# Seven output products with four sums, in tiles 1 to 8: another form of the fast output product in a sparse-attention and bilinear-FFN kernel

## The chip, the cores and the metric

The kernel runs on one core of a Trainium2 chip. The metric is the device time of one execution in microseconds (us); the median of the runs is compared. PE is the matrix engine, PEld its weight load, DVE the vector engine, ACT the scalar engine, POOL the GpSimd engine and SP the engine that issues DMAs.

## The reference

The inputs are q, k, v of shape (8, 8, 576, 64) and the weights w_a, w_b (512 x 1536) and w_out (1536 x 512), all in float32.

```python
scores = scale * np.matmul(q, k.transpose(0, 1, 3, 2))
mask_local = (rel >= 0) & (rel < 32)
mask_strided = (rel >= 0) & (pos[None, :] % 32 == pos[:, None] % 32)
scores = np.where(masks, scores, -1e9)      # first 4 heads local, last 4 strided
attn = softmax(scores); attn_out = attn @ v
x = attn_out.transpose(0, 2, 1, 3).reshape(4608, 512)
out = ((x @ w_a) * (x @ w_b)) @ w_out       # 4608 x 512, float32
```

## The kernel before

The 4608 tokens are cut into nine tiles (t = 0 to 8) of 512 tokens, and a tile into 16 slots, numbered 16t to 16t+15. In slots 0 to 11 (`ffn_ab`, f = 0 to 11) PE makes 128 columns of d_ff of `x @ w_a` and `x @ w_b` in two PSUM banks a and b, four matmuls of 512 columns each (L581). ACT copies a to SBUF (L598), and DVE multiplies it with b into `pf[:, f]` (L601 where the tile uses the fast output product, with the tokens sorted into two halves; L603 elsewhere). Slots 12 to 15 make the output, `pf` times `w_out`.

The plain output product (`ffn_y`, tiles 0 and 1) makes 4 x 12 matmuls of 512 columns (L768). Each of the four results is copied by ACT (L777) and stored. The fast one (`ffn_ys`, tiles 2 to 8, named by `FAST_Y`) sees the output as two by two blocks: two halves of the tokens (i), two halves of the 512 output columns (j), and the two halves (e) of each pair of d_ff chunks. Seven products of 128 x 256 blocks replace eight. Each has 2 x 6 matmuls of 256 columns (q = two interleaved sets of tokens, g = six chunk pairs; L686), 84 a tile. Some operands are sums: `wf` holds sums of weight blocks, made once by `fast_w` (L175), and `pss` holds sums of `pf` blocks, made in each tile by `fast_s` (L614 to L618) on DVE. `y_plan` runs this for tiles 2 to 7 and `y_tail` for tile 8. `post` moves the products out of four banks a, b, c, d in the order 3, 4, 1, 7, 5, 2, 6: three ACT copies (L658, L669, L671), four DVE additions (L662, L665, L667, L675), and two POOL subtractions that are put into slots 16t+15 and 16t+17 (L881 is where `do` queues them).

The banks of `mm_bank` go round: three buffers of the pool "mm" and one of "tp", so every fourth request gets the same bank. A request waits until all readers of the bank's last contents are done.

The attention of the later batches is mixed in between the matmuls. A table (`STEPS` for batches 1 and 2, `LATER` for 3 to 7) gives the slot of each step, relative to 16(b-1). A step S makes scores on PE (L385), Exp on ACT (L393) and a mask on DVE (L403). A step V makes `o` on PE (L486), Ln and Exp of the sums on ACT (L495, L496), and two multiplications into `xT` on DVE (L500 or L502). Both have one PSUM tile for all steps. `step_D` transposes q and k of a coming batch on DVE (L327, L332). Steps with a .5 position run in the middle of a slot. In the output phase each of the four slots takes 21 matmuls from the generator, with the step of a .5 position after 11 of them; slot 15 takes the rest. For tiles 2 to 6 the steps around the output phase are V4 after slot 9, S6 after 10, V5 after 11, S7 after 12, V6 within 13, V7 after 14, and S0 of the next batch after 15. In tile 1, V4, V5, V6, V7 lie within slots 28, 29, 30, 31, and S6, S7 after 28 and 29.

The order on every engine is that of the program (`manual_schedule`). The main loop runs a slot, then what `soon` holds for it, then the table's steps (`take(i)`), then what `at` holds for it, in the order in which it was put in:

```python
            done = fn(t, j, mid) if fn is not ffn_ab else fn(t, j, mid, first.get(j) if t == 0 else None)
            if i > 13 and i in at and done is not None:
                nc.gpsimd.tensor_copy(pace, done)
            for f in soon.get(i, ()):
                f()
            take(i)
            for f in at.get(i, ()):
                f()
```

The copy into `pace` (L936) holds POOL, and with it the loads that POOL issues, until the slot's result is there.

Of the kernel before, what the change touches and what calls it, by code (L numbers as in the profile page):

```python
# [7 lines left out]
F32 = mybir.dt.float32  # L8
# [18 lines left out]
FAST_Y = (2, 3, 4, 5, 6, 7, 8)  # L27
# [3 lines left out]
def kernel(  # L31
# [136 lines left out]
    wf = wp.tile([128, 5, FG, HN], BF16, name="wf")  # L168
    wov = wo_sb.rearrange("p (g e) (j n) -> p e j g n", e=2, j=2)

    def fast_w(n, gs):
        a, b, op = ((wov[:, 0, 1], wov[:, 1, 1], ALU.subtract), (wov[:, 1, 0], wov[:, 0, 0], ALU.subtract),
                    (wov[:, 0, 0], wov[:, 1, 1], ALU.add), (wov[:, 0, 0], wov[:, 0, 1], ALU.add),
                    (wov[:, 1, 0], wov[:, 1, 1], ALU.add))[n]
        nc.vector.tensor_tensor(wf[:, n, gs], a[:, gs], b[:, gs], op=op)  # L175
# [349 lines left out]
    def step_X(b, c):  # L525
# [17 lines left out]
                 12.6: "S1", 12.75: "L0 X2", 13: "s2 X3 V0 m2 L1 W3", 13.5: "V1 S3 W4", 14: "V2 X0", 14.5: "V3 D1", 15: "X1"},  # L543
# [64 lines left out]
    def fast_s(t, n, gs):  # L608
        if t not in pss:
            pss[t] = nat.tile([128, FG * 5 * SW], BF16, tag="shared", name="ps").rearrange("p (n g m) -> p n g m", g=FG, n=5)  # L610
        s = pss[t][:, :, gs, :HT]
        x = pfs[t].rearrange("p (g e) (i m) -> p e i g m", e=2, i=2)[:, :, :, gs]
        if n == 0:
            nc.vector.tensor_tensor(s[:, 0], x[:, 0, 0], x[:, 1, 1], op=ALU.add)  # L614
        elif n == 1:
            nc.vector.tensor_tensor(s[:, 1:3], x[:, 0], x[:, 1], op=ALU.add)
        else:
            nc.vector.tensor_tensor(s[:, 3:], x[:, :, 1], x[:, :, 0], op=ALU.subtract)  # L618
# [4 lines left out]
    def products(t):  # L623
        pf, s = pfs[t], pss[t]
        full = lambda e, i: (lambda g, q: pf[:, 2 * g + e, HT * i + q:HT * (i + 1):2])
        summed = lambda n: (lambda g, q: s[:, n, g, q:HT:2])
        wsum = lambda n: (lambda g: wf[:, n, g])
        wfull = lambda e, j: (lambda g: wov[:, e, j, g])
        return {"3": ("a", full(0, 0), wsum(0)), "4": ("b", full(1, 1), wsum(1)), "1": ("c", summed(0), wsum(2)),
                "2": ("b", summed(2), wfull(0, 0)), "5": ("a", summed(1), wfull(1, 1)), "6": ("c", summed(3), wsum(3)),  # L630
                "7": ("d", summed(4), wsum(4))}

    def f32t(nm):
        return fsb.tile([128, 2, HN], F32, tag=nm, name=nm, bufs=1)
# [10 lines left out]

    def y_plan(t):

        plan, bank, v = products(t), {}, {}
        y = []

# [4 lines left out]
        def post(k):  # L655
            if k == "3":
                v["a"] = v["w"] = f32t("ya")
                nc.scalar.copy(v["a"], bank["a"])  # L658
                y.extend(y_bufs())
                v["y"] = y  # L660
            elif k == "4":
                nc.vector.tensor_tensor(v["w"], bank["b"], v["a"], op=ALU.add)  # L662
            elif k == "1":
                v["e"] = f32t("ye")
                nc.vector.tensor_tensor(v["e"], bank["c"], v["w"], op=ALU.add)  # L665
            elif k == "7":
                nc.vector.tensor_tensor(v["e"], v["e"], bank["d"], op=ALU.subtract)  # L667
            elif k == "2":
                nc.scalar.copy(y[1][:, :, col(0)], bank["b"])  # L669
            elif k == "5":  # L670
                nc.scalar.copy(y[0][:, :, col(1)], bank["a"])  # L671
                do(16 * t + 15, nc.gpsimd.tensor_tensor, y[0][:, :, col(0)], v["e"], y[0][:, :, col(1)], ALU.subtract)
                do(16 * t + 18, store_half, 0)
            else:
                nc.vector.tensor_tensor(v["w"], bank["c"], v["w"], op=ALU.add)  # L675
                do(16 * t + 17, nc.gpsimd.tensor_tensor, y[1][:, :, col(1)], v["w"], y[1][:, :, col(0)], ALU.subtract)
                do(16 * t + 19, store_half, 1)

        for k in "3417526":
            b, lhs, rhs = plan[k]  # L680
            new = b not in bank
            if new:
                bank[b] = mm_bank([128, 2, HN])
            for q in range(2):
                for g in range(FG):
                    nc.tensor.matmul(bank[b][:, q], lhsT=lhs(g, q), rhs=rhs(g), start=new and q == 0 and g == 0,  # L686
                                     stop=g == FG - 1, skip_group_check=True)
                    if g == FG - 1 and q == 1:
                        post(k)
                    yield v  # L690

    def y_tail(t):

        plan, y = products(t), y_bufs()
        w, e = f32t("ya"), f32t("ye")
        v = {"a": w, "y": y}
        for q in range(2):
            if q == 0:
                bank = {x: mm_bank([128, HN]) for x in "abcd"}
            else:  # L700
                bank = {"a": psum4["o"].tile([128, 2, 512], F32, tag="o", name="end")[:, 0, :HN],
                        "b": pst.tile([128, 2, 512], F32, tag="st", name="end")[:, 0, :HN],
                        "c": mm_bank([128, HN]), "d": mm_bank([128, HN])}
            c21, c12, c22 = y[1][:, q, col(0)], y[0][:, q, col(1)], y[1][:, q, col(1)]
            wq, eq = w[:, q], e[:, q]
            seen = set()
            for k in ("3415267", "3412567")[q]:
                b, lhs, rhs = plan[k]
                cuts = [(slice(0, HN), bank[b])]
                if (k, q) == ("7", 1):  # L710
                    cuts = [(slice(0, 128), bank[b][:, :128]), (slice(128, HN), mm_bank([128, 128]))]
                for n, dst in cuts:
                    for g in range(FG):
                        nc.tensor.matmul(dst, lhsT=lhs(g, q), rhs=rhs(g)[:, n], start=g == 0 and b not in seen,  # L714
                                         stop=g == FG - 1, skip_group_check=True)
                        if g < FG - 1:
                            yield v
                    if k == "3":
                        nc.scalar.copy(wq, bank["a"])
                    elif k == "4":  # L720
                        nc.vector.tensor_tensor(wq, bank["b"], wq, op=ALU.add)
                        if q == 0:
                            fast_s(t, 1, slice(FG - 1, FG))
                    elif k == "1":
                        nc.vector.tensor_tensor(eq, bank["c"], wq, op=ALU.add)
                        if q == 0:
                            fast_s(t, 2, slice(FG - 1, FG))
                    elif k == "2":
                        nc.scalar.copy(c21, bank["b"])
                        nc.gpsimd.tensor_tensor(wq, wq, c21, op=ALU.subtract)  # L730
                        if q == 1:
                            y_store(nc.sync, t, y, 1, q, col(0))
                    elif k == "5":
                        nc.scalar.copy(c12, bank["a"])
                        nc.gpsimd.tensor_tensor(eq, eq, c12, op=ALU.subtract)
                        if q == 1:
                            y_store(nc.scalar, t, y, 0, q, col(1))
                    elif k == "6":
                        nc.vector.tensor_tensor(c22, bank["c"], wq, op=ALU.add)
                        y_store(nc.sync, t, y, 1, q, col(q) if q else slice(0, d_model))  # L740
                    else:
                        nc.vector.tensor_tensor(y[0][:, q, n], eq[:, n], dst, op=ALU.subtract)
                        if q == 0:
                            y_store(nc.sync, t, y, 0, q)
                        else:
                            y_store(nc.scalar if n.start == 0 else nc.sync, t, y, 0, q, n)
                    yield v
                seen.add(b)

    def ffn_ys(t, j, mid):  # L750
        if j == 0:
            yst[t] = (y_tail if t == NT - 1 else y_plan)(t)
        for i in range(21):
            v = next(yst[t])
# [5 lines left out]
        return (v["a"][:1, 0, :1], None, v["y"][0][:1, 0, HN:HN + 1], v["y"][1][:1, 0, :1])[j]  # L760
# [36 lines left out]
    with tc.manual_schedule(engines={ENG.PE, ENG.SP, ENG.Pool, ENG.DVE, ENG.Activation}):  # L797
# [85 lines left out]
        soon = {16 * t + 11: [lambda t=t: fast_s(t, 0, slice(2, 6))] for t in FAST_Y[:-1]}  # L883
# [34 lines left out]
        for n, slot in enumerate((16, 16, 19, 20, 22)):  # L918
            do(slot, fast_w, n, slice(3, 6))
        for g in range(FG):  # L920
            for n in range(3 if g < FG - 1 else 1):
                do(16 * (NT - 1) + 2 * g + 1, fast_s, NT - 1, n, slice(g, g + 1))
        for t in FAST_Y[:-1]:
            for slot, n, z0, z1 in ((4, 0, 0, 2), (6, 2, 0, 2), (8, 1, 0, 2), (10, 2, 2, 4), (11, 2, 4, 6),
                                    (12, 1, 2, 6)):
# [44 lines left out]
```

## Time and profile before

| | |
|---|---|
| median of 3 runs | 328.86 us (328.71 to 328.89) |
| span of the profiled execution, first to last instruction | 326.3 us; its own device time is not given apart from the runs |
| mean granted PE clock | 0.999 |
| PE busy | 320.6 us (98%) |
| DVE busy | 265.7 us (81%) |
| ACT busy | 202.7 us (62%) |
| POOL busy | 177.2 us (54%) |
| output phases: tile 1 / tile 3 / tile 7 | 80.17 to 92.11 / 150.19 to 160.16 / 283.19 to 292.36 us |

The profile is of one execution. Each row of a timeline gives the start in us from the span's start, the duration, the engine, the line, the operation and its tiles; what stands in square brackets is idle time ahead of it and what ended it. Rows of one engine overlap a little, so the step from one start to the next is the cost in a full queue. PE matmuls are pipelined: a row of 0.27 us for 256 columns follows its predecessor by 0.11 us.

### The profile page before, as it was taken

To read this page: it belongs to the slowest core of one execution; us is meant where nothing else is said; L and a number is where in the kernel's file an instruction comes from. 1 tells how busy PE (TensorE), PEld (TensorE's weight loads), DVE (VectorE), ACT (ScalarE), POOL (GpSimd) and SP (SyncE) were. 2 spreads that over 40 slices of the span, in tenths; PEclk is the share of its full clock that TensorE was granted. 3 is DMA by queue.
4 is the path that set the end of the run, shared out by engine and by line. 5 is a ranking of instruction groups with operands and counts; after the bars stand their busy time and mean duration, and the time that the engine had idled before them with its cause. 6 is when DMAs were issued, how large, how long until landed. Compare 5 with 4: busy or idle time off the path is not lost.

```text
span 326.3 us, 7676 instructions
## 1 busy us (share of the span) xinstructions
PE 320.6 (98%) x2820; PEld 205.5 (63%) x2820; DVE 265.7 (81%) x509; ACT 202.7 (62%) x329; POOL 177.2 (54%) x295
## 2 busy tenths in 40 slices
PE   8999999999999999999999999999999999999995
PEld 6754655455555587557999985569555954584474
DVE  6766888889778999999999999999877845647562
ACT  6764775478778765777677757875677643313321
POOL 8935839599966655875577557853312031232021
PEclk9999999999999999999999999999999999999999
DMA  9999999999999798799979999898033022004004
GB/s 151 154 204 201 204 184 182 173 171 136 132 213 116 95 97 79 77 217 125 83 72 199 138 86 77 160 180 84 20 77 115 2 67 64 0 2 129 1 2 129
DMA packets 98869, 37.50 MB, mean 115 GB/s; under 512 B 76688, under 2 KB 96016, under 8 KB 98832
## 3 DMA queue, kind: packets, MB, share of 16 engines
q0 software_dynamic: 85968, 19.48, 64.5%
q1 hardware_dynamic: 12576, 17.34, 18.4%
q8 instruction: 22, 0.36, 0.4%
q10 hardware_dynamic: 288, 0.20, 0.2%
q14 instruction: 15, 0.12, 0.1%
HBM read 39.51 MB, written 9.44 MB: 150 GB/s over the span
## 4 chain that ended last, share of the span: by engine, by line
PE 96%; DMA 2%; POOL 0%; DVE 0%; issue 0%; POOLq 0%; ACT 0%; DVEq 0%
PE mm L581 56%; PE mm L686 17%; PE mm L768 6%; PE st L385 5%; PE o L486 4%; DMA shared<-in_q_dram 2%; PE mm L714 2%; PE o L442 1%; PE ab L581 1%; PE misc L154 1%; PE tp L511 1%; PE tp L296 1%; PE end L714 1%; PE tp L287 0%; POOL shared L197 0%
## 5 line engine op out<-in xcount | busy, mean ns | idle before, releaser
L581 PE MATMUL mm<-xT,wa_sb 128*128 128x512 bf16 (+1 forms) x472 | 110.3, 357 | 0.0
L581 PE MATMUL mm<-xT,wb_sb 128*128 128x512 bf16 (+1 forms) x472 | 110.3, 357 | 0.0
L598 ACT COPY a_sb<-mm 128x512 f32<-128x512 f32 x106 | 62.1, 586 | 48.3 <-PE mm L581 47.6
L936 POOL CAST pace<-pf 1x1 f32<-1x1 bf16 x84 | 31.4, 374 | 84.0 <-DVE pf L601 80.7
L581 PEld LDWEIGHTS <-wb_sb 128*128 128x128 bf16 x480 | 46.3, 98 | 44.0 <-issue 0.2
L601 DVE TENSOR_TENSOR pf<-a_sb,mm 128x512 bf16<-128x512 f32 x84 | 56.4, 672 | 17.0 <-PE mm L581 13.8
L581 PEld LDWEIGHTS <-wa_sb 128*128 128x128 bf16 x480 | 42.7, 98 | 31.3
L393 ACT ACTIVATE p<-st 128x576 bf16<-128x576 f32 (+1 forms) x64 | 41.6, 650 | 11.7 <-PE st L385 11.1
L495 ACT ACTIVATE xr<-o 64x576 f32<-64x576 f32 x48 | 31.1, 649 | 25.0 <-PE o L486 24.2
L686 PEld LDWEIGHTS <-ps 128*128 128x128 bf16 x360 | 34.6, 98 | 3.9
L496 ACT ACTIVATE xr<-xr 64x576 f32<-64x576 f32 x48 | 32.9, 685 | 1.5
L500 DVE TENSOR_TENSOR xT<-o,xr 64x288 bf16<-64x288 f32 x48 | 21.5, 447 | 7.2 <-ACT xr L496 6.7
L502 DVE TENSOR_TENSOR xT<-o,xr 64x288 bf16<-64x288 f32 x48 | 21.5, 448 | 6.2 <-ACT xr L496 5.1
L686 PE MATMUL mm<-wf,ps 128*128 128x256 bf16 x216 | 26.4, 273 | 0.0
L768 PE MATMUL mm<-wo_sb,pf 128*128 128x512 bf16 x96 | 23.4, 379 | 0.0
L403 DVE TENSOR_TENSOR p<-p,mask_l 128x576 int16<-128x576 int16 x32 | 22.2, 694 | 1.2 <-ACT p L393 1.1
L243 POOL DMA_DIRECT2D vs<-in_v_dram x24 | 19.7, 821 | 3.0 <-PE st L385 2.2
L212 POOL DMA_DIRECT2D kl<-in_k_dram x24 | 16.1, 671 | 5.5 <-issue 3.6
L212 POOL DMA_DIRECT2D ql<-in_q_dram x24 | 16.0, 666 | 5.2 <-DMA wo_sb<-in_moe_w_out_dram 3.8
L603 DVE TENSOR_TENSOR pf<-a_sb,mm 128x512 bf16<-128x512 f32 x22 | 14.9, 676 | 4.3 <-ACT a_sb L598 2.8
L936 POOL COPY pace<-y_sb 1x1 f32<-1x1 f32 x16 | 2.8, 177 | 27.8 <-ACT y_sb L669 15.1
L686 PE MATMUL mm<-wf,pf 128*128 128x256 bf16 x144 | 17.6, 273 | 0.0
(162 smaller groups left out, 502.1 us busy)
## 6 DMA issues: line engine op xcount, KB each, us to landing
out_dram<-y_sb SPq DMA_DIRECT2D x12, 512.0 KB, 4.6
out_dram<-y_sb SPq DMA_DIRECT2D x10, 256.0 KB, 3.3
vl<-in_v_dram POOLq DMA_DIRECT2D x6, 384.0 KB, 6.8
kl<-in_k_dram POOLq DMA_DIRECT2D x24, 72.0 KB, 3.0
ql<-in_q_dram POOLq DMA_DIRECT2D x24, 72.0 KB, 3.0
vs<-in_v_dram POOLq DMA_DIRECT2D x24, 72.0 KB, 3.7
wo_sb<-in_moe_w_out_dram POOLq DMA_DIRECT2D x4, 384.0 KB, 9.2
natk<-in_k_dram POOLq DMA_DIRECT2D x20, 72.0 KB, 3.3
```

Of the source, the lines that this page charges most:

```text
L212: nc.gpsimd.dma_start(out=t[32 * h:32 * h + 32], in_=src[b, h].rearrange("(i y) d -> y i d", y=32))
L393: nc.scalar.activation(p[:M, :, :W], st[:M, :, :W], ACT.Exp, scale=scale)
L403: nc.vector.tensor_tensor(pi, pi, mk, op=ALU.bitwise_and)
L495: nc.scalar.activation(r, sums, ACT.Ln)
L496: nc.scalar.activation(r, r, ACT.Exp, scale=-1.0)
L500: nc.vector.tensor_mul(dst[:, W * half:W * (half + 1)], o[:64, j, :W], r[:, j])
L581: nc.tensor.matmul(ps_[:, c0:c0 + n], lhsT=w[:, kk, 128 * f:128 * (f + 1)], rhs=xT[:, kk, x0:x0 + n], start=(kk == first and c0 == 0), sto ...
L598: nc.scalar.copy(a_sb, ab[0])
L601: nc.vector.tensor_mul(pf[:, f, :].rearrange("p (i a s) -> p a i s", i=2, s=16), halves(a_sb), halves(ab[1]))
L686: nc.tensor.matmul(bank[b][:, q], lhsT=lhs(g, q), rhs=rhs(g), start=new and q == 0 and g == 0, stop=g == FG - 1, skip_group_check=True)
L768: nc.tensor.matmul(ybank[j], lhsT=pf[:, f, 128 * j:128 * (j + 1)], rhs=wo_sb[:, f], start=(f == 0), stop=(f == FD - 1))
L936: nc.gpsimd.tensor_copy(pace, done)
```

## The change

The fast output product is used in tile 1 too. Its form is another. Instead of five sums of `pf` blocks and five of weight blocks there are four of each, some made from an earlier sum, and all are subtractions or additions of two blocks. Three PSUM banks X, Y, Z take the seven products in the order 1, 7, 6, 4, 5, 2, 3, where X holds 1, then 1+6, then 1+6+5, then 1+6+5+3, and is copied by ACT at each of these points; Z holds 7, copied, and then 7+4; Y holds 2. A tile's output phase thus has five ACT copies and three DVE additions, one of them (after 5) from SBUF alone, and no POOL subtraction. The places of the sums in the slots change: s0, s2, s1 of the first four chunk pairs are made after slots 8, 9, 10, the last two pairs of s2, s0, s1 directly after slot 11's `pf`, and s3 after slots 11 and 12. The tail tile mixes the products of q = 0 and q = 1.

```diff
-FAST_Y = (2, 3, 4, 5, 6, 7, 8)
+FAST_Y = (1, 2, 3, 4, 5, 6, 7, 8)
...
-    wf = wp.tile([128, 5, FG, HN], BF16, name="wf")
+    wf = wp.tile([128, 4, FG, HN], BF16, name="wf")
...
+        a, b = ((wov[:, 0, 1], wov[:, 0, 0]), (wov[:, 1, 1], wf[:, 0]), (wov[:, 1, 1], wov[:, 0, 1]),
+                (wov[:, 1, 0], wf[:, 1]))[n]
+        nc.vector.tensor_tensor(wf[:, n, gs], a[:, gs], b[:, gs], op=ALU.subtract)
...
-        if n == 0:
-            nc.vector.tensor_tensor(s[:, 0], x[:, 0, 0], x[:, 1, 1], op=ALU.add)
-        elif n == 1:
-            nc.vector.tensor_tensor(s[:, 1:3], x[:, 0], x[:, 1], op=ALU.add)
-        else:
-            nc.vector.tensor_tensor(s[:, 3:], x[:, :, 1], x[:, :, 0], op=ALU.subtract)
+        a, b, op = ((x[:, 0, 1], x[:, 1, 1], ALU.add), (s[:, 0], x[:, 0, 0], ALU.subtract),
+                    (x[:, 0, 0], x[:, 0, 1], ALU.subtract), (x[:, 1, 0], s[:, 1], ALU.subtract))[n]
+        nc.vector.tensor_tensor(s[:, n], a, b, op=op)
...
+        return {"1": ("X", full(0, 0), wfull(0, 0)), "2": ("Y", full(1, 0), wfull(1, 0)), "3": ("X", summed(3), wfull(1, 1)),
+                "4": ("Z", full(1, 1), wsum(3)), "5": ("X", summed(0), wsum(0)), "6": ("X", summed(1), wsum(1)),
+                "7": ("Z", summed(2), wsum(2))}
...
+    def y_post(k, y, q, bank, n=slice(0, HN)):
+        part = lambda i, j: y[i][:, q, HN * j:HN * (j + 1)]
+        if k in "1765":
+            nc.scalar.copy({"1": part(0, 0), "7": part(0, 1), "6": part(1, 0), "5": part(1, 1)}[k], bank)
+        if k == "4":
+            nc.vector.tensor_tensor(part(1, 0), bank, part(1, 0), op=ALU.add)
+        elif k == "5":
+            nc.vector.tensor_tensor(part(1, 1), part(1, 1), part(0, 1), op=ALU.add)
+        elif k == "2":
+            nc.vector.tensor_tensor(y[0][:, q, n], bank, y[0][:, q, n], op=ALU.add)
+        elif k == "3":
+            nc.scalar.copy(part(0, 1), bank)
...
+        bank = {x: mm_bank([128, 2, HN]) for x in "YXZ"}
...
-        for k in "3417526":
+        for k in "1764523":
             b, lhs, rhs = plan[k]
             for q in range(2):
                 for g in range(FG):
+                    nc.tensor.matmul(bank[b][:, q], lhsT=lhs(g, q), rhs=rhs(g), start=k in "172" and q == 0 and g == 0,
                                      stop=g == FG - 1, skip_group_check=True)
                     if g == FG - 1 and q == 1:
+                        y_post(k, y, slice(0, 2), bank[b])
+                    yield y
+        do(16 * t + 18, store_half, 0)
+        do(16 * t + 19, store_half, 1)
...
+        for q, k in ((0, "1"), (0, "7"), (0, "6"), (0, "4"), (0, "5"), (1, "1"), (0, "3"), (1, "7"), (1, "6"), (0, "2"),
+                     (1, "5"), (1, "4"), (1, "3"), (1, "2")):
...
-        return (v["a"][:1, 0, :1], None, v["y"][0][:1, 0, HN:HN + 1], v["y"][1][:1, 0, :1])[j]
+        return (y[0][:1, 0, :1], None, y[1][:1, 0, HN:HN + 1], y[1][:1, 0, :1])[j]
...
-        soon = {16 * t + 11: [lambda t=t: fast_s(t, 0, slice(2, 6))] for t in FAST_Y[:-1]}
+        soon = {16 * t + 11: [lambda t=t, n=n: fast_s(t, n, slice(4, 6)) for n in (2, 0, 1)] for t in FAST_Y[:-1]}
...
-            for slot, n, z0, z1 in ((4, 0, 0, 2), (6, 2, 0, 2), (8, 1, 0, 2), (10, 2, 2, 4), (11, 2, 4, 6),
-                                    (12, 1, 2, 6)):
+            for slot, n, z0, z1 in ((8, 0, 0, 4), (9, 2, 0, 4), (10, 1, 0, 4), (11, 3, 0, 4), (12, 3, 4, 6)):
                 do(16 * t + slot, fast_s, t, n, slice(z0, z1))
```

In the table of steps for batch 1 the fifth weight sum's step (W4) goes, and so does its second half in slot 22.

## The prediction

> **What bounds the kernel now.** I read the page first: the busy shares, and the chain that ended last.
>
> ```profile
> PE 320.6 (98%) x2820; PEld 205.5 (63%) x2820; DVE 265.7 (81%) x509; ACT 202.7 (62%) x329; POOL 177.2 (54%) x295
> ...
> PE 96%; DMA 2%; POOL 0%; DVE 0%; issue 0%; POOLq 0%; ACT 0%; DVEq 0%
> ```
>
> PE is the path for 96% of the span. The waits view shows under 2 us of PE waiting in all, and the PE timeline has no hole inside a tile. So less PE work is gained one for one, and every new PE wait is lost one for one. Next I took the windows of three output phases (columns: window and its length, then busy time and count of PE, PEld, DVE, ACT, POOL, clock, DMA share, GB/s): tile 1 with the plain product, tile 5 and tile 7 with seven products.
>
> ```profile
> 80.20:92.10 11.90, 11.90 (x97) 6.16 (x96) 8.65 (x17) 8.60 (x15) 10.00 (x15) 1.00 1.34 140
> ...
> 218.65:228.60 9.95, 9.95 (x112) 8.99 (x111) 9.71 (x18) 6.42 (x10) 4.94 (x9) 1.00 0.70 77
> ...
> 283.40:292.50 9.10, 9.10 (x85) 8.12 (x84) 5.19 (x7) 1.76 (x3) 2.35 (x4) 1.00 0.01 2
> ```
>
> Where attention steps are mixed in (tile 5) DVE is full; in tile 7, where they have ended, it is half empty. What decides is thus whether DVE and ACT meet the deadlines that the new form sets in tiles 1 to 6.
>
> **The gain.** In the PE timeline six plain 512-column matmuls of L768 take 80.17 to 81.46 us, 0.216 each, 48 of them 10.38 us. Twelve 256-column ones (L686, 291.05 to 292.36) take 1.31, so one takes 0.109 and a product of twelve 1.31; 84 take 9.17. Tile 1 gains 1.21 us. Tiles 2 to 8 keep 84: no PE gain.
>
> **Three new deadlines.** (a) Before, four banks served seven products, and a bank came back after three others; now X is used by products 1, 6, 5, 3, with only one product (1.31 us) between 1 and 6, between 6 and 5, and between 5 and 3, and PE must wait until ACT has copied X. (b) The banks go round in a ring of four, so Y, X, Z are the banks of f=10's a, f=10's b, f=11's a. The first product needs X: DVE must have done pf of f=10 when the phase begins; before, that bank was the second product's. The second product now needs sum s2, whose last two groups come after pf of f=11. (c) Y is read last by a DVE addition, and the next tile's first b product takes that bank.
>
> **Tile 5 as the pattern of 2 to 5.** From the DVE timeline (start, duration):
>
> ```profile
> 216.11 0.91 DVE L502 TENSOR_TENSOR xT<-o,xr 64x288 bf16<-64x288 f32 x2
> 217.05 0.78 DVE L327 STREAM_TRANSPOSE tq<-ql 128x576 bf16<-128x576 bf16 x1
> 217.75 0.65 DVE L601 TENSOR_TENSOR pf<-a_sb,mm 128x512 bf16<-128x512 f32 x1
> 218.33 0.44 DVE L403 TENSOR_TENSOR p<-p,mask_s 72x576 int16<-72x576 int16 x1
> 218.69 0.68 DVE L618 TENSOR_TENSOR ps<-pf 128x1024 bf16<-128x1024 bf16 x1
> 219.29 0.68 DVE L601 TENSOR_TENSOR pf<-a_sb,mm 128x512 bf16<-128x512 f32 x1
> 220.00 0.69 DVE L614 TENSOR_TENSOR ps<-pf 128x1024 bf16<-128x1024 bf16 x1
> ```
>
> PE begins the phase at 218.48. The multiplications of step V4 start when ACT's Exp is done, in all these tiles 2.37 to 2.41 us before the phase. DVE is in order, so work saved ahead of them doesn't help what follows. Slot 9 now adds s2 of four groups ahead of pf of f=10. A sum of 128x1024 takes 0.61 from start to start (218.69 to the next row), so pf starts at 217.75+0.61=218.36 and ends at 219.01. No row shows what PE needs after that; the bounds are 0 and 0.15 (ACT starts 0.02 after its own last row, and 0.2 after PE), and I take 0.05. Product 1 starts at 219.06: **0.58 lost**. Mask 218.94, s1 of four groups for L618's place 219.30, pf of f=11 219.90, s2's last 512 columns 0.71 later (219.29 to 220.00) and 0.41 long (L614's 128x512 form): 221.02, with 0.05 221.07. PE wants it 16 matmuls after its start, at 219.06+1.75=220.81: **0.26**.
>
> ACT in the same tile, and the end of the phase on DVE:
>
> ```profile
> 222.70 0.65 ACT L495 ACTIVATE xr<-o 64x576 f32<-64x576 f32 x1 [0.81 <-PE o L486]
> 223.38 0.69 ACT L496 ACTIVATE xr<-xr 64x576 f32<-64x576 f32 x1
> ...
> 226.37 0.65 ACT L495 ACTIVATE xr<-o 64x576 f32<-64x576 f32 x1
> ```
>
> ```profile
> 228.72 0.71 DVE L332 STREAM_TRANSPOSE tk<-natk 128x512 bf16<-128x512 bf16 x1
> 229.35 0.65 DVE L675 TENSOR_TENSOR ya<-mm,ya 128x512 f32<-128x512 f32 x1
> ```
>
> Step V6 lies four matmuls before product 6 ends; PE goes on from it at 222.50. Its Ln and Exp stand ahead of the copy of 6 on ACT: Exp ends at 224.07, the copy (0.59) at 224.68, PE may go on at 224.73. Product 5 would start 4+12 matmuls after 222.50, at 224.25: **0.48**. (The copy of 7 has Exp of S7 ahead of it and is done 0.4 early; the copy of 5 is ahead of V7's Ln, early too.) PE goes on from V7 at 226.15. The addition of 2 takes the place of L675, behind V7's multiplications and L332, at 229.35, done 230.00, with 0.05 230.05. The next tile's b product begins at 229.35: **0.70**. Sum 2.02 a tile, 8.1 for four, since each wait comes after the one before and nothing on PE takes it back.
>
> **Tile 6** has no transposes. V4 starts at 250.13, 0.94 later s2, then pf of f=10 ends at 252.33, before the phase at 252.51: nothing. s2's end, by the same rows 254.41, against 254.26: 0.15. The copy of 6: 0.48. The addition of 2 straight behind V7's multiplications, 3.25 after V7 against 2.94 (21 matmuls' 2.29 and 0.65): 0.31. Sum 0.94.
>
> **Tile 7** has only copies on ACT: the copy of 6 is done 0.5 early; s2 at 1.45 against 1.75. Nothing.
>
> **Tile 1** is new to the sums, and DVE there is late already. pf of f=10 and f=11 now start at 79.42 and 81.97; s0 and s2 come ahead of the first, s1 too ahead of the second. First: 79.42+1.22=80.64, done 81.29, product 1 at 81.34 against 80.17: 1.17. Second: 81.97+1.83=83.80, s2 from 84.51 to 84.92, against 81.34+2.00 (16 matmuls and V4's 0.26): 84.97, 1.63. V4's multiplications stand behind s2, s0, s1 (0.33 each), a transpose (0.76) and s3 (0.61): 86.87 to 87.80. Step V5 needs its PSUM tile at 86.97: 0.86. Copies behind Ln and Exp: 0.22 and 0.16, V7's tile 0.1. Waits 4.14, less the gain 1.21: +2.93.
>
> **Tail (tile 8).** The same 84 matmuls; 0.13 for s2's last group (DVE 314.36 against 314.28), the copies of 128x256 take 0.37 and end some 0.02 to 0.3 before their bank is wanted. The last addition and two 64 KB stores stay. I take 0.1, with bounds -0.2 (the addition of L742 no longer stands behind L739) and +0.5 (a 128 KB store's issue of 0.61 ahead of the last on ACT's queue).
>
> **What costs nothing.** Five copies for three on ACT (+1.17 a tile; ACT 62%), one addition from SBUF alone (no row; 0.35 to 0.69 by half and whole of L662; DVE waits for Exp behind it), a fifth weight sum less (2x0.55), pace copies of slots 14 and 30 behind that addition: loads that land in 3 us and are used slots later. Two POOL subtractions a tile go (1.27 each). Beside one of them the mask L403 took 1.97 us in place of 0.44, so 1.5 of DVE come back at a tile's start; V4's wait for Exp swallows it.
>
> [...]
>
> **Sum:** 8.1+0.94+2.93+0.1=12.1. The span of 326.3 is 2.6 under the median of the runs, 328.86, taken as fixed: 328.86+12.1=341.0.
>
> **Rivals.** *Only ACT's waits are real* (0.14): the DVE relief reaches the deadlines after all. Then 5x0.48=2.4 in tiles 2 to 6 and 0.54+0.22+0.16=0.9 for the copies of 1, 6 and 5 in tile 1, less 1.21: 331.0. For it: a tile's sums fall from 5.0 us of DVE (L614's 0.42 and 0.69, three of L618 and one of L616 at 0.68, L616's 1.19) to 4x0.69+4x0.42=4.4, its additions by 0.7, and the 1.5. Against it: V4 starts on Exp in each tile. *Faster* (0.09): X's copies come in time, because ACT reaches the copy of 6 before V6's Ln, and DVE is ahead: 328.86-1.21=327.65. The place is product 5 in tiles 2 to 6; it decides where that wait is under 0.2 a tile and DVE's under 0.05. The code order speaks against it. *The waits do more* (0.12): PE is slow to restart, 0.15 rather than 0.05 at some 24 waits (+2.4), and late steps push the next tile's: 345 to 348. The clock is 1.00 in every window of the trace.
>
> [...]
>
> *No change* (0.03): waits just eat the 1.21.
>
> **Numbers.** The forecast holds 0.62. Its own range: without (c) and the 0.05s about 337, with 0.15 each 343.5. For eight in ten I reach to the ACT rival and a part of the worse one: 331 to 345. 0.2% (0.66 us) is about what a measurement tells from none; faster 0.09, within 0.03, slower 0.88.
>
> **Right or wrong.** Tile 1's phase should take about 14.9 us instead of 11.9, tiles 2 to 5 about 2 more each, tile 7 the same. PE waits on pf L601 at the start of the phase, on ps within product 7, on ACT's copy before product 5, on DVE's addition in the next tile's f=0. If tile 5's phase stays at 9.97 and tile 1's falls to 10.7, the order on ACT and DVE is not what I read.

## The result, and the profile after

The changed kernel takes 337.88 us (median of 4 runs, 337.25 to 338.55) against 328.88 for the kernel before: ratio 1.0276 (95% interval 1.0256 to 1.0296), 9.0 us slower. The span of the profiled execution goes from 326.3 to 335.9 us. The forecast was 341.0, with a range of 331 to 345.

The page's busy times first. PE's is nearly what it was (320.6 before) in a span that is 9.6 us longer; DVE's has fallen from 265.7 although tile 1 makes sums now.

```profile
PE 321.0 (96%) x2825; PEld 207.7 (62%) x2856; DVE 254.4 (76%) x522; ACT 210.6 (63%) x346; POOL 154.6 (46%) x269
```

So the change did relieve DVE and did not give PE more to do: the loss is PE waiting. The windows of the output phases of tiles 1, 5 and 7, with the columns as before:

```profile
80.35:95.10 14.75, 12.23 (x140) 9.69 (x140) 13.59 (x27) 9.42 (x16) 9.89 (x13) 1.00 0.98 99
225.50:236.90 11.40, 10.52 (x114) 8.99 (x113) 9.71 (x21) 7.11 (x12) 5.45 (x9) 1.00 0.59 67
292.13:301.40 9.27, 9.27 (x86) 8.29 (x85) 4.79 (x9) 2.35 (x4) 0.70 (x2) 1.00 0.01 2
```

Tile 1's phase grew from 11.9 to 14.75 us and PE is idle for 2.5 of them, tile 5's from 9.95 to 11.40; tile 7's is as it was (the two windows, 9.10 and 9.27, are cut by hand; counted as in the table below it is 9.28 in both). The clock column stays at 1.00 (after it DMA share and GB/s). The waits view names PE's waits (us in total, times, longest; the start-to-start loss of a wait is longer than this idle time, 0.68 for 0.52 in tile 2's product 7, as the row of the last matmul is 0.27 long and the step to the next 0.11):

```profile
PE mm L666 <- DVE ps L614: 3.2, 4, 1.6
PE mm L666 <- ACT y_sb L643: 1.6, 5, 0.3
...
PE mm L580 <- DVE y_sb L649: 0.7, 2, 0.5
PE o L485 <- DVE xT L501: 0.7, 1, 0.7
PE mm L666 <- DVE pf L600: 0.4, 1, 0.4
```

L666 is the products' matmul, L614 a sum, L643 the copy of a bank, L649 the addition of 2, L501 the multiplications of a step V, L600 pf. In the kernel before no row of this kind was there. Counted from the first weight load of a phase to the first of the next, this is where the span's 9.55 us lie:

| | before | after | |
|---|---|---|---|
| output phase of tile 1 | 12.37 | 14.74 | +2.37 |
| of tiles 2, 3, 4, 5 | 10.21 each | 11.41, 11.41, 11.37, 11.42 | +4.77 |
| of tile 6 | 9.88 | 10.43 | +0.55 |
| of tile 7 | 9.28 | 9.28 | 0 |
| slots 0 to 11 of tiles 3 and 7 | 23.82, 20.61 | 24.52, 20.98 | +1.07 |
| tile 8 from its output on, last store included | 13.45 | 14.11 | +0.66 |

The rest is 0.1. One phase, tile 2's, shows the two waits that tiles 2, 4 and 5 have alike; in tile 3 the first of them is split, 0.57 ahead of product 1 (pf of f=10) and 0.16 at s2. First the DVE timeline around its start, then the PE timeline, then ACT's:

```profile
117.95 0.65 DVE L614 TENSOR_TENSOR ps<-pf 128x1024 bf16<-128x1024 bf16 x1
118.52 0.68 DVE L600 TENSOR_TENSOR pf<-a_sb,mm 128x512 bf16<-128x512 f32 x1
...
119.48 0.68 DVE L614 TENSOR_TENSOR ps<-ps,pf 128x1024 bf16<-128x1024 bf16 x1
120.08 0.67 DVE L600 TENSOR_TENSOR pf<-a_sb,mm 128x512 bf16<-128x512 f32 x1
120.68 0.75 DVE L614 TENSOR_TENSOR ps<-pf 128x512 bf16<-128x512 bf16 x2
```

```profile
118.68 1.51 PE L666 MATMUL mm<-wo_sb,pf 128*128 128x256 bf16 x12
120.03 0.60 PE L666 MATMUL mm<-wf,ps 128*128 128x256 bf16 x4
121.14 0.72 PE L666 MATMUL mm<-wf,ps 128*128 128x256 bf16 x5 [0.52 <-DVE ps L614]
...
123.86 1.47 PE L666 MATMUL mm<-wf,pf 128*128 128x256 bf16 x12
125.65 0.60 PE L666 MATMUL mm<-wf,ps 128*128 128x256 bf16 x4 [0.31 <-ACT y_sb L643]
```

```profile
123.62 0.65 ACT L494 ACTIVATE xr<-o 64x576 f32<-64x576 f32 x1 [0.34 <-PE o L485]
124.31 0.69 ACT L495 ACTIVATE xr<-xr 64x576 f32<-64x576 f32 x1
125.01 0.59 ACT L643 COPY y_sb<-mm 128x512 f32<-128x512 f32 x1
```

Product 7 stops after four matmuls. The fifth wants s2 of the last groups, the first of the two sums in the row at 120.68, ready at about 121.09; PE goes on at 121.14. Where the next matmul would have come at 120.46, 0.68 us are lost. Product 5 would start at 125.17; the copy of 6 stands behind the Ln and Exp of V6, ends at 125.60, and PE goes on at 125.65: 0.48 lost. Both show 0.05 us from the end of the releasing row to PE.

### The profile page after: what moved, and what is told of

Read it like the earlier page. It is cut to its first block, busy times and chain, and to the rows that moved or that the text cites. A ratio compares the mean times of both kernels' runs of the same rounds, so it can differ in the third digit from the quotient of the medians.

```text
span 335.9 us, 7659 instructions
## 1 busy us (share of the span) xinstructions
PE 321.0 (96%) x2825; PEld 207.7 (62%) x2856; DVE 254.4 (76%) x522; ACT 210.6 (63%) x346; POOL 154.6 (46%) x269
## 5 line engine op out<-in xcount | busy, mean ns | idle before, releaser
L580 PE MATMUL mm<-xT,wa_sb 128*128 128x512 bf16 (+1 forms) x451 | 107.7, 356 | 1.1
L892 POOL CAST pace<-pf 1x1 f32<-1x1 bf16 x77 | 26.2, 341 | 122.9 <-DVE pf L600 122.7
L600 DVE TENSOR_TENSOR pf<-a_sb,mm 128x512 bf16<-128x512 f32 x96 | 64.8, 675 | 22.3 <-PE mm L580 16.0
L666 PEld LDWEIGHTS <-ps 128*128 128x128 bf16 x336 | 31.5, 98 | 10.9 <-DVE ps L614 4.7
L666 PE MATMUL mm<-wf,ps 128*128 128x256 bf16 x252 | 32.9, 273 | 4.8 <-DVE ps L614 3.2
L643 ACT COPY y_sb<-mm 128x512 f32<-128x512 f32 (+1 forms) x32 | 17.8, 557 | 16.2 <-PE mm L666 13.4
L501 DVE TENSOR_TENSOR xT<-o,xr 64x288 bf16<-64x288 f32 x48 | 21.6, 449 | 7.9 <-ACT xr L495 7.3
L666 PEld LDWEIGHTS <-pf 128*128 128x128 bf16 x252 | 23.7, 98 | 4.1 <-issue 0.5
L666 PE MATMUL mm<-wo_sb,pf 128*128 128x256 bf16 x168 | 21.9, 273 | 0.4 <-DVE pf L600 0.4
L614 DVE TENSOR_TENSOR ps<-pf 128x1024 bf16<-128x1024 bf16 (+2 forms) x40 | 17.5, 464 | 0.0
L202 POOL DMA_DIRECT2D natk<-in_k_dram x24 | 14.5, 607 | 2.1 <-issue 2.1
```

Source lines behind the costliest of these rows:

```text
L501: nc.vector.tensor_mul(dst.rearrange("d (p r) -> d p r", r=RS)[:, :, G * half:G * (half + 1)], o[:64, j, :W].rearrange("d (g p) -> d p g", ...
L580: nc.tensor.matmul(ps_[:, c0:c0 + n], lhsT=w[:, kk, 128 * f:128 * (f + 1)], rhs=xT[:, kk, x0:x0 + n], start=(kk == first and c0 == 0), sto ...
L600: nc.vector.tensor_mul(pf[:, f, :].rearrange("p (i a s) -> p a i s", i=2, s=16), halves(a_sb), halves(ab[1]))
```

## The experiments

Theory (the order theory): each lost microsecond is a single wait of PE, set by the order of the work on DVE and ACT and by the bank that a request is given. Its main rival (the load theory): DVE and ACT have too much to do, so that another order would only move the waits. In the diffs `...` stands for what is unchanged.

**plain1: is tile 1 the whole loss?**

```diff
-FAST_Y = (1, 2, 3, 4, 5, 6, 7, 8)
+FAST_Y = (2, 3, 4, 5, 6, 7, 8)
```

> The new form in tiles 2 to 8 alone, tile 1 by the plain product again. Order theory (each lost microsecond is one wait of PE that the order on DVE, ACT or the banks sets): tile 1's phase of 14.74 us goes back to about 12.37, so 2.4 under the changed kernel: 335.5 (335.0 to 336.0), and tiles 2 to 6 lose as much as they did. Rival, load (DVE and ACT have too much to do from tile 1 on, and tile 1's extra work is handed on to the later tiles): 333 or less. Rival, the new form is harmless and tile 1 is the whole loss: 329.

Measured 334.88 us, ratio to before 1.0172 (1.0124 to 1.022), just under the expected range. Tile 1's phase is 12.40 again; the phases of tiles 2 to 6 are 11.42, 11.41, 11.37, 11.41 and 10.42, as they were. Neither rival holds: tile 1 costs some 3 us of time (2.3 in its phase), hands nothing on to the later phases, and the form alone costs the rest.

**copies_first: the copy ahead of Ln and Exp.**

```diff
-            if i == 10:
+            if i == (12, 14, 17, 10)[j]:
                 mid()
```

> The middle step of an output slot is issued after the product's copy: after 12, 14+1, 17+1 matmuls in the first three slots in place of 11, so that ACT has the copy of 1, 6, 5 ahead of a step V's Ln and Exp. Order theory: the 0.48 us ahead of product 5 goes in tiles 2 to 6, and 0.23 and 0.15 in tile 1: 2.8 less, 335.1 (334.7 to 335.6). Load theory: ACT has the same work, the wait turns up at the next copy or at the multiplications of V6 and the time stays within 0.5 of 337.9.

Measured 336.55 us, ratio 1.0217 (1.0172 to 1.0262): 1.3 less, not 2.8. The phases split this. Tiles 2 to 5 take 10.91 to 10.96 and tile 6 takes 9.97, each 0.46 less, as the order theory had it. The waits view of this run has no row of PE waiting for ACT's copy (L643), and s2's is left:

```profile
PE mm L666 <- DVE ps L614: 3.4, 4, 1.8
PE o L485 <- DVE xT L501: 1.5, 2, 1.2
```

In tile 1, where all three middle steps were moved, the phase grew from 14.74 to 15.19: V6 now came seven matmuls later and V7 not, so V7 waited 1.38 us for the PSUM tile after 0.12 before, while V5's wait fell from 0.86 to 0.42 (the second line holds both, 1.2 and 0.3 of idle time; the 0.7 of the changed kernel was V5's). In this tile the wait moved on rather than went.

**sums_early: the sums where DVE is idle.**

```diff
-... fast_s(t, n, slice(4, 6)) for n in (2, 0, 1)]
+... fast_s(t, n, slice(z, 6)) for n, z in ((2, 4), (0, 4), (1, 0))]
...
-((8, 0, 0, 4), (9, 2, 0, 4), (10, 1, 0, 4), (11, 3, 0, 4), (12, 3, 4, 6))
+((7, 2, 0, 4), (8, 0, 0, 4), (11, 3, 0, 4), (12, 3, 4, 6))
```

> s2 and s0 of the first four groups after slots 7 and 8 (where DVE is idle 0.7 us ahead of each step V) in place of 8 and 9, and the whole s1 after slot 11 in one piece, so nothing stands between V4 and pf of f=10 and f=11 but the transpose and the mask. Order theory: the 0.68 to 0.73 us ahead of or within product 7 goes in tiles 2 to 5, and about 1.1 of the 1.78 in tile 1: 3.9 less, 334.0 (333.4 to 334.7). Load theory: DVE's work is the same, so the time stays within 0.5 of 337.9.

Measured 335.48 us, ratio 1.0181 (1.0129 to 1.0233): 2.4 less of the 3.9. Tiles 2 to 5 fell from 11.4 to 10.82, 11.04, 10.74 and 10.82, with the same work on DVE: that much is order. Left are 0.11 in tiles 2 and 5 for s1, now one longer operation of 0.96 us, and in tile 3 0.37 for X. Tile 1 gained 0.67 of 1.1. Its wait for s2 fell from 1.78 to 0.99, but V5's wait for its PSUM tile rose from 0.86 to 1.20, as s3 and the longer s1 stand ahead of V4's multiplications. The two lines of the waits view change their places against the run above:

```profile
PE mm L666 <- ACT y_sb L643: 1.6, 5, 0.3
...
PE mm L666 <- DVE ps L614: 0.8, 1, 0.8
```

**tail_split: the last stores.**

```diff
-                if k == "5" and q == 0 or (q, k) == (1, "4"):
+                if k == "5" and q == 0:
                     y_store(nc.sync, t, y, 1, q)
+                elif (q, k) == (1, "5"):
+                    y_store(nc.sync, t, y, 1, q, col(1))
+                elif (q, k) == (1, "4"):
+                    y_store(nc.sync, t, y, 1, q, col(0))
```

> The tail's last 256 KB store (second half of the tokens, q = 1) is cut into two of 128 KB, the first issued one product earlier. If the 0.65 us that the tail lost is a burst of stores at the end: 0.3 to 0.6 less, 337.3 to 337.6. If it lies in the compute of the tail, or in the fixed way of the last store: within 0.15 of 337.9.

Measured 337.64 us, ratio 1.0251 (1.0204 to 1.0299), which alone tells nothing. In the trace tile 8 takes 13.60 us from its output on, after 14.11, and 13.45 before. The other traces agree: 14.01 to 14.13 in the four other runs that store as the changed kernel does, 13.49 to 13.68 in the five later ones that store as this one. The landing times of the tail's stores, first of the changed kernel, then of this run:

```profile
DMA to landing us min/median/max: 2.7/2.8/2.9
```

```profile
DMA to landing us min/median/max: 2.2/2.4/2.8
```

(2.2/2.4/2.9 before.) The compute of the tail was not late in either: the last DVE row ends 9.7 us after the first product in both, and 9.9 in the kernel before. The last three stores are issued at the same times in both, counted from the first product, 9.8 us for the last. The last one took 2.77 us to land behind a 256 KB store and 2.33 behind its two halves, of which the first was issued 0.33 us earlier. So some 0.4 us of the tail's loss lies in those stores; cutting the large one and starting it earlier were not tried apart.

**bank_turn: who gets which bank.** In the built program (the program shows the banks, the trace does not) "mm" takes PSUM banks 2 to 4 and "tp" bank 5, and the banks do not go round as a ring of four. "tp" has one buffer, and every fourth request gets it; of "mm" a request is given any of the three. In tile 2 X was bank 3, f=11's a, and in tile 3 bank 5, f=10's b. After tile 2 both Y and the next b were bank 5; after tiles 3, 4 and 5 b was not Y's bank. In the changed kernel's timeline the b product waits for the addition of 2 after tile 2; after tile 3 it starts together with an addition that is as late:

```profile
130.75 0.65 DVE L649 TENSOR_TENSOR y_sb<-mm,y_sb 128x512 f32<-128x512 f32 x1
131.45 0.81 PE L580 MATMUL mm<-xT,wb_sb 128*128 128x512 bf16 x3 [0.54 <-DVE y_sb L649]
...
166.68 0.65 DVE L649 TENSOR_TENSOR y_sb<-mm,y_sb 128x512 f32<-128x512 f32 x1
166.68 0.82 PE L580 MATMUL mm<-xT,wb_sb 128*128 128x256 bf16 x6
```

```diff
+        used[0] += 1
         do(16 * t + 18, store_half, 0)
         do(16 * t + 19, store_half, 1)
```

> One line: each output phase counts a fourth bank request, so the pool "tp", which has one buffer, never falls to Y or X, and the next tile's b product is given another bank than Y. Theory: the wait of the first b product on the addition of 2 is there only where Y and b are both the "tp" bank (0.71 us after tile 2, 0.37 after tile 6), and the wait of product 1 on pf of f=10 only where X is (tile 3). Both boundary waits go, tile 3's 0.57 turns into a longer wait for s2: 1.1 less, 336.8 (336.3 to 337.2). Rival, these waits are DVE's lateness whatever the bank: 337.9.

Measured 337.41 us, ratio 1.0259 (1.024 to 1.0278). The wait after tile 2 is gone (23.82 us for tile 3's slots 0 to 11 again), and tile 3 now loses 0.69 at s2 and nothing at X. The one after tile 6 stayed (20.98), since Y and the next b fell on one "mm" bank there. So 0.7 of the 1.1. The mechanism holds: the wait needs both, the late addition and the shared bank. After tiles 1 and 7 of this run Y and the next b share a bank too, but the addition is on time and nothing waits. In the waits view L649's row falls from 0.7 (two waits) to:

```profile
PE mm L580 <- DVE y_sb L649: 0.2, 1, 0.2
```

plain1 shows the same with the banks left to themselves. Its plain tile 1 asks for one bank more, which in the built program puts Y and the next b on bank 5 after tile 3 and not after 2, and X on bank 5 in tile 4 and not in 3. Its waits moved along: none after tile 2, 0.69 after tile 3 (the row below), none after tile 6, and X's 0.53 stands in tile 4.

```profile
165.84 0.38 PE L580 MATMUL mm<-xT,wb_sb 128*128 128x256 bf16 x2 [0.53 <-DVE y_sb L649]
```

**all_order: everything at once.** The four edits above (of the middle steps only V6 in tiles 2 to 6) and s3 in one piece:

```diff
-            if i == 10:
+            if i == (14 if t > 1 and j == 1 else 10):
...
-... (11, 3, 0, 4), (12, 3, 4, 6)):
+... (13, 3, 0, 6)):
```

> All changes of order together, the same arithmetic in the same tiles: sums early, s3 in one piece after slot 13, the copy of 6 ahead of V6 in tiles 2 to 6, the fourth bank request, the split store. Order theory: the waits of tiles 2 to 6 go (2.3 for the copies, 2.3 for the sums, 1.4 for the banks), 0.5 of the tail, and of tile 1 some 0.7 for the sums and 0.6 for V4's multiplications that no longer stand behind s3: 7.7 less than 337.88, about 330.2 (329.6 to 331.0), and what is left over 328.86 is tile 1, where DVE is full. Load theory: DVE and ACT hold PE up whatever the order: 334 or more.

Measured 333.02 us, ratio 1.0141 (1.0105 to 1.0177): under the load theory's 334, but 2.8 over the forecast. The PE rows tell why. In tiles 2 to 5 product 3 now waits 0.33 for s3, which I had put too late; the addition of 2 after tile 6 costs 0.52; in tile 1 V5's wait for its tile fell from the 1.20 of sums_early to 0.60 as expected, but V7's rose from 0.12 to 0.68 and the phase is 14.03 for 14.07. There the later s3 only moved the wait, as the load theory has it.

**all_order_plain1: the same with tile 1 plain.**

> The same with tile 1 by the plain product: the new form in tiles 2 to 8. Order theory: no wait is left, PE has just the work of the kernel before, so the time is that of the kernel before: 328.9 (328.5 to 329.5). That the new form also saves time (fewer sums, no POOL subtraction) as DVE is relieved: under 328.2. Load theory: 331 or more.

Measured 331.02 us, ratio 1.0063 (1.0046 to 1.008). That is 2.1 over the order theory's 328.9 and the value that the load theory gave, so the time alone speaks for the rival. The PE rows name other waits: again the 0.33 for s3 in four tiles, 0.11 in three of them at s1, and the 0.52, together 2.2. The next run decides whether the place of s3 made them.

**order_plain1_b: s3 back in slots 11 and 12.**

> As the run before with tile 1 plain, but s3 back after slots 11 and 12, since the run before lost 0.33 us ahead of product 3 in each of tiles 2 to 5, waiting for s3. Order theory: 1.3 less than 331.02, 329.7 (329.2 to 330.2); what is left over 328.9 is 0.11 a tile for s2, and the first b product after tile 6. Rival, DVE hands the wait on, to V6 or the addition of 2: 330.6 or more.

Measured 329.40 us (10 runs), ratio 1.0019 (1.0004 to 1.0033), as the order theory had it. PE's waits view has no row of L666 left; of the new form there is the one wait after tile 6:

```profile
PE misc L154 <- PEq L915: 0.9, 1, 0.9
...
PE mm L580 <- DVE y_sb L649: 0.2, 1, 0.2
```

With four sums, five copies and three banks, tiles 2 to 8 thus cost 0.5 us more than the old form (0.1 to 1.1 by the interval). The load theory falls for these tiles.

**order_c: the same order with tile 1 by the new form (the diff is against all_order).** In tile 1 s3 is made in one piece after slot 13, as in all_order: its piece after slot 12 is empty (`z0` and `z1` are both 4), so it is not split there as the expectation says.

```diff
-... (13, 3, 0, 6)):
-                do(16 * t + slot, fast_s, t, n, slice(z0, z1))
+... (11, 3, 0, 4 if t > 1 else 0), (12, 3, 4, 6 if t > 1 else 4), (13, 3, 0, 0 if t > 1 else 6)):
+                if z1 > z0:
+                    do(16 * t + slot, fast_s, t, n, slice(z0, z1))
```

> The new form in tiles 1 to 8 with the order mended: s3 after slots 11 and 12 in tiles 2 to 7, after 12 and 13 in tile 1. Order theory: 1.3 less than 333.02, 331.7 (331.2 to 332.3), and tile 1 at about 14.0 us is nearly all that is left. Rival: 332.6 or more.

Measured 331.67 us, ratio 1.0091 (1.0076 to 1.0106). Against the run above tile 1's phase costs 14.03 for 12.36. This is the best order that I found with tile 1 in the new form, and it is slower than the kernel before.

**old_form_tile1: the kernel before, its own form in tile 1 too.**

```diff
-FAST_Y = (2, 3, 4, 5, 6, 7, 8)
+FAST_Y = (1, 2, 3, 4, 5, 6, 7, 8)
```

> The kernel before with its own form of the seven products used in tile 1 too. DVE in tile 1 is late already: pf of f=11 goes from 81.97 to about 83.2, which product 4 wants at 82.4 (1.5 lost), and V4's multiplications stand behind two more sums (1.2 lost for V5's tile): 2.7 less the gain of 1.21: 330.4 (329.6 to 331.2). Rival, the old form with its later deadlines could have had the 1.21: 327.7; then the loss in tile 1 is of the new form and not of the tile.

Measured 331.45 us, ratio 1.008 (1.0061 to 1.0099), just over the expected range. Tile 1's phase is 14.62, where the changed kernel has 14.74: five sums, four banks and other deadlines cost the same. Product 4 waits 1.14 for pf, and three V steps 2.27 for their PSUM tile. So the old form could not have had the 1.21 there either, in its own order.

**pool_sums1: DVE relieved by POOL.** As order_c, with two sums of tile 1 on POOL:

```diff
-        nc.vector.tensor_tensor(s[:, n], a, b, op=op)
+        eng = nc.gpsimd if (t, gs.start, n) in ((1, 0, 0), (1, 0, 2)) else nc.vector
+        eng.tensor_tensor(s[:, n], a, b, op=op)
```

> As order_c, but in tile 1 the first four groups of s2 and s0 are made on POOL in place of DVE (1.2 us less for DVE there, the rest as it is). If DVE's lateness is what tile 1 loses, its waits for s2 (0.99) and for V5's PSUM tile (0.6) shrink by up to 1.2 and tile 1 takes about 12.9 us: 330.6. Rival: DVE waits for POOL as the masks did in the kernel before (1.97 in place of 0.44 us beside a POOL subtraction of 1.28), or the loads behind POOL come late: tile 1 at 14 us or more, 331.7 or more.

Measured 332.97 us, ratio 1.0132 (1.0114 to 1.0149): 1.3 slower than order_c, as the rival had it. Tile 1's phase is 16.16 for 14.03, and its slots 0 to 11 take 0.4 less. The POOL and DVE timelines of that run:

```profile
77.73 2.14 POOL L615 TENSOR_TENSOR ps<-pf 128x1024 bf16<-128x1024 bf16 x1
...
81.20 2.13 POOL L615 TENSOR_TENSOR ps<-pf 128x1024 bf16<-128x1024 bf16 x1
```

```profile
78.60 2.50 DVE L402 TENSOR_TENSOR p<-p,mask_s 72x576 int16<-72x576 int16 x1
81.03 0.76 DVE L326 STREAM_TRANSPOSE tk<-kl 128x576 bf16<-128x576 bf16 x1
```

The mask (0.45 else) starts while POOL's sum is running and ends 1.2 us after it, while POOL's next rows (a pace copy at 79.80 and two DMA issues of L202, the last ending at 81.18) are still under way; which of them held the mask, the trace doesn't tell. A DMA issue by itself does not: in the changed kernel 21 masks start while POOL issues one, and each takes 0.41 to 0.46. Beside the second POOL sum a transpose, pf and a step V's multiplications run in their usual 0.76, 0.64 and 0.90; of what ran beside the two sums only the mask was lengthened. DVE lost 2.05 us to save two sums of some 0.6 each, pf of f=10 ended at 82.36 and product 1 waited 1.47 for it. Whether DVE in tile 1 could be relieved in another way was not tried.

## Why the prediction was right, and where its steps were off

The direction, the kind of loss and the tiles were right; the size was 12.1 forecast and 9.0 measured (9.55 of span). By the steps of the forecast:

- **The gain of 1.21 in tile 1** was made and outweighed: the rows there show some 3.5 us of waits, and 2.37 net. Forecast 4.14 and 2.93.
- **s2 within product 7, tiles 2 to 5**: together with X 0.84 forecast, 0.68 to 0.73 measured. The end of s2 was nearly right (in tile 2 2.41 us after the phase began, 2.54 forecast for tile 5, 221.02 − 218.48). The split was wrong: the 0.58 ahead of product 1 came in tile 3 alone, as X had another bank elsewhere. That matters little, since PE waits for the end of s2 either way.
- **The copy of 6 behind V6's Ln and Exp**: 0.48 forecast, 0.48 measured in five tiles, and 0.46 recovered by the order alone.
- **The addition of 2 ahead of the next b product**: the step that failed. 0.70 was forecast after each of tiles 2 to 5 and 0.31 after 6, 3.1 in all; measured 0.71 after tile 2, none after 3 to 5, 0.37 after 6. DVE's lateness was as forecast (the row at 166.68 to 167.33 after tile 3), but b had another bank. I took "every fourth request gets the same bank" for the whole pool; it holds for "tp" alone. This one term was 2.0 too large.
- **The first product in tile 1 waiting for pf of f=10 (1.17)**: the same step. X was f=10's a there, and only the last chunk pair's data was late: 0.14, then 0.25 for V4's tile. s2 was 1.78 for 1.63, V5's tile 0.86 for 0.86, the later copies 0.23 and 0.15 for 0.22 and 0.16.
- **The tail**: 0.1 forecast, 0.66 measured, just outside its bounds. I looked at the queues' issue and not at the landing of the last store, 2.77 us behind a 256 KB store here and 2.33 behind its halves in tail_split. Counted to that store's landing the loss is 0.4 (12.40 before, 12.81 after); the rest lies behind the landing, where the kernel before took 1.05 us and old_form_tile1, with the same tail, 1.46.
- **What costs nothing** held: the two copies more as work for ACT, the addition of 5 (0.69 us) and the pace copies show no wait on PE beyond those named above, where a copy stands behind Ln and Exp. In the kernel before, masks beside a POOL subtraction took 1.47 to 2.26 us early in tiles 3, 4 and 5, two in each; without the subtractions none takes over 0.46. So 2.5 to 2.8 us of DVE come back in each of these three tiles (1.5 was forecast, from one mask) and none in the others. PE gained nothing from it (slots 0 to 11 of tiles 4 and 5 take 24.06 and 23.82 us before and after): DVE waits for Exp, 0.7 to 0.9 us ahead of each V step in tile 3's slots 1 to 7.
- **PE's restart**, taken as 0.05 within 0 and 0.15, is 0.05 in the rows above and 0.06 at product 1 of tile 3 (pf ends at 155.12, PE goes on at 155.18). The clock is 1.00 in the changed kernel's window of tile 1, which holds a wait of 1.6 us, and its mean is 0.999 in copies_first, with one of 1.8; the worse rival is out.
- The rival that only ACT's waits are real falls by the rows of s2.

## What to carry to other kernels

Fewer operations on an engine that is not the path saved nothing here, while each shorter deadline on it could cost: before changing the order of products, write down for each PSUM bank and each sum who must be done by which matmul, and walk the consumer's queue with the durations of the trace. Look the buffers up in the built program; which buffer a pool hands out is a thing to read and not to derive. A wait from order can be mended by order (copies_first, sums_early: 0.46 and 0.4 to 0.6 us a tile in tiles 2 to 5 for no work saved). In tile 1 the orders tried mostly moved the waits from one step to the next (14.74, 15.19, 14.07 and 14.03 us), with DVE busy for 12.8 of the 14.03 in order_c; that DVE is too full there for any order is likely and not shown.

## What the runs showed of the hardware that was not expected

- A DVE mask that started 0.87 us into a POOL sum of 2.14 us took 2.50 us in place of 0.45 and ended 1.2 us after POOL's row; POOL went straight on with a copy and two DMA issues until 81.18, and the trace does not tell how much of the mask's time belongs to which. Masks that start during a DMA issue alone took 0.41 to 0.46.
- The last stores of 64 KB landed 2.70 and 2.77 us after their issue behind a 256 KB store, and 2.25 and 2.33 us when that one was cut in two and begun 0.33 us earlier.
